# Moving zero products about on TensorE in a fused attention and soft-MoE kernel: three out at the front, ten in at the end

## The chip, the cores and the metric

The kernel runs on one core of a Trainium2 chip. That core has a matrix engine (TensorE, in the profile PE, with its weight loads as PEld), a vector engine (VectorE, DVE), a scalar engine (ScalarE, ACT), a general engine (GpSimd, POOL), a queue for DMAs (SyncE, SP) and 16 DMA engines that all queues share. The metric is the device time of one execution in microseconds; less is better. Each engine works through its own list of instructions in order and waits on semaphores that the others raise.

## The reference

Four sequences of 768 positions go through an attention of 8 heads of 64 columns. Some heads attend to all earlier keys, the others only to 4 "sink" keys and a window of 64. The result, 3072 rows of 512 columns, goes through a soft mixture of experts: each of 32 slots is a softmax-weighted mean over all rows, eight experts of two layers work on four slots each, and each row is a softmax-weighted sum of the slots' results. The core of it:

```python
scores = np.where(mask, q @ k.T / 8, -1e9)           # per head; mask: causal, or sink + window
a = exp(scores - max); a = a / a.sum(-1)             # softmax over the keys
x = (a @ v), heads side by side                      # 3072 x 512
logits = x @ phi                                     # 3072 x 32
slot_input = softmax(logits, over rows).T @ x        # 32 x 512
h = relu(slot_input[e] @ w1[e]); slot_out[e] = h @ w2[e]   # 8 experts, 4 slots each
return softmax(logits, over slots) @ slot_out        # 3072 x 512, float32
```

Inputs and output are float32; the DMAs that POOL issues turn the loads into bf16 on the way, and PE multiplies bf16. The two layers' weights are 32 MB of float32, q, k and v 19 MB, the output 6 MB.

## The kernel before

The attention is cut into 16 "pairs" p = 4b + n of a sequence b and two heads, n and n + 4. For each pair PE makes score blocks (QK), ACT takes their exponentials (EX) into a buffer `pt`, DVE multiplies the blocks that need it by a mask (MK), and PE multiplies by the values (PV.p.i for the six query blocks i = 0 to 5). DVE normalises the result (NM: a reciprocal at L831, then a product at L833), PE transposes it (XT, L845) and DVE or ACT copies the transposes to SBUF (XE). The last pair is cut in halves: PV.15.0 to PV.15.2 go to the first of the two PSUM banks of `pvb`, PV.15.3 to PV.15.5 to the second, and NM.15.0, XT.15.0, XE.15.0 work on the first half, NM.15.3, XT.15.3, XE.15.3 on the second. XT.15.0 and XT.15.3 share one PSUM buffer.

Behind that come the logits of the last sequence (LG), the slots' sums (DS, SA, SI), the first layer (H, L1017), its transposes, and the second layer (W2.e for expert e, L1055). The second layer's last two experts are cut into column halves: W2.6.0 and W2.7.0 make the left 256 columns, W2.6.1 and W2.7.1 the right ones. Each half is scaled into SBUF (SO.0, SO.1; L1113), multiplied with the mixing weights on PE (OM, L1130), scaled by ACT or DVE (OE, L1138 and L1140), and stored (ST, L1149). Twelve of the 24 row tiles go out in left and right halves, the other twelve whole, after the right half is there.

The loads are one queue. POOL issues them in a written order, with waits for the buffers they go to; the last four are the weight halves w14.0, w15.0, w14.1 and w15.1 (L347), for W2.6.0, W2.7.0, W2.6.1 and W2.7.1. SP issues nearly all stores.

The order of everything is made once, when the program is built: a planner (`Plan.run`) places the operations with given costs, start keys and hand-tuned shifts, and the engines' lists follow its order. What an operation emits is not seen by the planner, only its given cost and its number of products.

Some operations emit products with a tile of zeros, `zt`, whose results nobody reads. `fill(n)` (L427) emits n products of 256 columns; TD (the products that make key positions, L432 and L433) begins with fifteen of them and ends with ten, and PE starts with these. ZG are five lone zeros in the first pairs (L511), Z five between the last steps of the slots (L1004). ZT0 and ZT1 (`wait_zeros`, L1073) emit three and two of 448 columns, ZT0 between W2.6.0 and W2.7.0, ZT1 between W2.6.1 and W2.7.1:

```python
def wait_zeros(name, n, key, dep, first=False):
    def emit_z(o):
        for _ in range(n):
            nc.tensor.matmul(banks[zw.slot][:, 0:448], ident, zt, start=True, stop=True)
```

Waits are put in by the framework, by buffers that an instruction writes and reads. For PSUM they can be coarser than the columns touched.

Of the kernel before, what the change touches and what calls it, by code (L numbers as in the profile page):

```python
# [151 lines left out]
def pe(ns, n=1):  # L152
    occ = ns * n / 1000.0
    return {"PE": (occ, occ + 0.27)}
# [72 lines left out]
def kernel(  # L227
# [13 lines left out]
    nc = tc.nc  # L241
# [30 lines left out]
    ident = sb.tile([P, P], BF16, name="ident")  # L272
# [8 lines left out]
    zt = sb.tile([P, 448], BF16, name="zt")  # L281
# [24 lines left out]
    trb = [ps.tile([P, 512], F32, name=f"tr{i}") for i in range(2)]  # L306
    pvb = ps.tile([P, 2, 512], F32, name="pv")

    def tr_bf(s, n):
        return trb[s].bitcast(BF16)[:, 0:n]  # L310
# [14 lines left out]
    def copy_engs(cols, rate=1.75):  # L325
        return {"DVE": (0.035 + cols / rate / 1000.0, 0.2 + cols / rate / 1000.0),
                "ACT": (0.07 + cols / 1200.0, 0.27 + cols / 1200.0)}

    def on(eng, occ, late=0.18):
        return {eng: (occ, occ + late)}  # L330

    def copy(o, dst, src):
        if o.eng == "ACT":
            nc.scalar.copy(dst, src)  # L334
        else:
            nc.vector.tensor_copy(dst, src)  # L336
# [88 lines left out]
    def fill(n):  # L425
        for _ in range(n):
            nc.tensor.matmul(pvb[:, 1, 0:256], zt[:, 0:128], zt[:, 0:256], start=True, stop=True)  # L427

    def emit_td(o):
        fill(15)  # L430
        t = trb[tdb.slot][:, 0:256]
        nc.tensor.matmul(t, unit[:, 0:128], tq, start=True, stop=False)  # L432
        nc.tensor.matmul(t, krow, unit, start=False, stop=True)  # L433
        fill(10)
# [70 lines left out]
    o_zt = pl.op("zt", on("DVE", 0.2), -100, lead=0.7, emit=lambda o: nc.vector.memset(zt, 0.0))  # L505
    tdb = Buf("TR")
    o_td = pl.op("TD", on("PE", 0.6, 0.3), -80, deps=[o_tab], acq=[tdb], emit=emit_td, mode="r32", mm=2)
    o_z = o_zt

# [179 lines left out]
    for b in range(B):  # L689
        for n in range(4):  # L690
            p = 4 * b + n
            k0 = T * p

            tr = Buf("TR")
# [83 lines left out]
    for b in range(B):  # L778
        for n in range(4):
            p = 4 * b + n  # L780
            k0 = T * p
            PVb[p] = Buf("PV")
            last = None
            iorder = [0, 1, 2, 3, 4, 5]

            def pv_at(h, i, p=p):
                return (h, 65 * i) if p < 15 else (i // 3, 195 * h + 65 * (i % 3))

            for i in iorder:
                deps, need = [v2e[p], vfo[p]] + [o_z][p:], set()  # L790
                for j in range(i + 1):
                    if (j, i) == (5, 5):
                        deps.append(exto[p])
                    else:
                        g = PGRP[(j, i)]
                        deps.append(masko[p, g] if i - j <= 1 else expo[p, g])

                def emit_pv(o, b=b, n=n, p=p, i=i, pv_at=pv_at):
                    pT = pTs[PTb[b, n].slot]
                    vb = vbs[VBb[b].slot]  # L800
                    for h in range(2):
                        bk, c = pv_at(h, i)
                        for j in range(i + 1):
                            rhs = vb[:, n, j, h, 0:65] if i - j <= 1 else vfs[VFb[p].slot][:, h, j, 0:65]
                            if (j, i) == (5, 5):
                                lt = ptx[PTXb[b].slot][:, h, n, :]
                            else:
                                lt = pT[:, h, PCOL[(j, i)]:PCOL[(j, i)] + 128]
                            nc.tensor.matmul(pvb[:, bk, c:c + 65], lt, rhs,  # L809
                                             start=(j == 0), stop=(j == i))  # L810

                last = pl.op(f"PV.{p}.{i}", pe(31.5, 2 * (i + 1)), k0 + T - 2.5 + 0.5 * i,
                             deps=list(dict.fromkeys(deps)) + ([last] if last else []),
                             acq=[PVb[p]] if i == 0 else [],
                             rel=[PTb[b, n]] + ([VFb[p]] if i == 5 else []) +
                                 ([PTXb[b], VBb[b]] if i == 5 else []), emit=emit_pv, mode="full", mm=2 * (i + 1))

            pvo = {i: pl.ops[i - 6] for i in range(6)}
            halves = [(0, 6)] if p < 15 else [(0, 3), (3, 6)]
            tr = Buf("TR")  # L820
            xhalf = {}
            for i0, i1 in halves:
                part = f"{p}" if i1 - i0 == 6 else f"{p}.{i0}"

                def emit_nm(o, i0=i0, i1=i1, b=b, n=n, p=p):
                    r = rs[p % 2][:, :, i0:i1]
                    if p < 15:
                        pvw = pvb[:, :, 65 * i0:65 * i1].rearrange("p i (j c) -> p i j c", c=65)
                    else:
                        pvw = pvb[:, i0 // 3, 0:390].rearrange("p (i j c) -> p i j c", i=2, c=65)  # L830
                    nc.vector.reciprocal(r, pvw[:, :, :, 64])  # L831
                    xo = xbs[XBb[b].slot][:, i0:i1, 128 * n:128 * (n + 1)].rearrange("p j (i d) -> p i j d", i=2)
                    nc.vector.tensor_tensor(xo, pvw[:, :, :, 0:64],  # L833
                                            r.rearrange("p i (j o) -> p i j o", o=1).to_broadcast([P, 2, i1 - i0, 64]),
                                            op=ALU.mult)

                normo[p] = pl.op(f"NM.{part}", on("DVE", 0.335 + 0.1333 * (i1 - i0)), k0 + T + 1.0,
                                 deps=[pvo[i1 - 1], XBb[b].op], acq=[XBb[b]] if n == 0 else [], rel=[PVb[p]],
                                 emit=emit_nm)

                def emit_xt(o, i0=i0, i1=i1, b=b, n=n, tr=tr):
                    t = tr_bf(tr.slot, 768)
                    xv = xbs[XBb[b].slot]
                    for i in range(i0, i1):
                        nc.tensor.transpose(t[:, 128 * i:128 * (i + 1)], xv[:, i, 128 * n:128 * (n + 1)], ident)  # L845

                a = pl.op(f"XT.{part}", pe(56, i1 - i0), k0 + T + 2.5, deps=[normo[p]],
                          acq=[tr] if i0 == 0 else [], rel=[XBb[b]], emit=emit_xt, mode="full", mm=i1 - i0)

                def emit_xe(o, i0=i0, i1=i1, n=n, tr=tr):  # L850
                    cs = slice(128 * i0, 128 * i1)
                    copy(o, xT[:, n, cs], tr_bf(tr.slot, 768)[:, cs])

                xhalf[i0] = xto[p] = pl.op(f"XE.{part}", copy_engs(128 * (i1 - i0)), k0 + T + 3.0, deps=[a, o_st, XTb[b].op],
                               acq=[XTb[b]] if n == 0 else [], rel=[tr], emit=emit_xe)
# [213 lines left out]

    def wait_zeros(name, n, key, dep, first=False):  # L1070
        def emit_z(o):
            for _ in range(n):
                nc.tensor.matmul(banks[zw.slot][:, 0:448], ident, zt, start=True, stop=True)  # L1073

        pl.op(name, pe(190, n), key, deps=[dep], acq=[zw] if first else [], rel=[zw], emit=emit_z, mode="full", mm=n)
# [89 lines left out]
    for gi in range(6):  # L1165
        n = dict(halved).get(gi, 0)
# [55 lines left out]
```

## Time and profile before

| | |
|---|---|
| median of 3 runs | 147.77 us (147.71 to 148.36) |
| profiled execution | 147.56 us |
| its span, first to last instruction | 145.8 us |
| PE busy | 124.6 us, 85% of the span |
| DVE, ACT, POOL busy | 110.8, 107.9, 40.5 us |
| moved by DMA | 33.40 MB, HBM read 52.49 MB, written 6.29 MB |
| mean granted TensorE clock | 0.944 |

A row of a timeline has the start in us from the span's first instruction, the duration, the engine, the line of the kernel, the operation, what it writes and reads, the shapes, and how many instructions are merged into the row; in brackets stands how long the engine was idle before it and what ended that. A row of a table of stretches has the stretch, its length, the busy time and number of instructions of PE, PEld, DVE, ACT and POOL, the granted TensorE clock (1.00 is full, 0.50 half), the mean busy share of the DMA engines and the GB/s moved. A row of the chain that ended last has start, duration, and the work; at each step it goes back to what released the next one. "DMA to landing" has the time from a DMA's issue until its data have landed: least, median, most of the DMAs in the stretch. In that view a line's row has durations in ns (least, median, most), and its first and last start.

### The profile page before, as it was taken

What the parts mean: (1) busy time and instruction counts of PE and PEld (TensorE: products, weight loads), DVE (VectorE), ACT (ScalarE), POOL (GpSimd) and SP (SyncE); (2) the same over time, 40 slices, a digit from 0 to 9 for tenths busy, and PEclk for the clock granted to TensorE, in tenths of its full rate; (3) what the DMA queues carried; (4) which work ended last, traced back from release to release, by engine and by line L of the source; (5) the groups of instructions that cost most, each with busy time, mean ns of one, the idle gap of its engine ahead of it and who ended that gap; (6) DMA issues with size and microseconds to landing.
All of it is one profiled execution on the core that took longest, in us unless ns stands there. A gap on an engine that the chain in (4) does not pass through costs nothing.

```text
span 145.8 us, 4941 instructions
## 1 busy us (share of the span) xinstructions
PE 124.6 (85%) x2134; PEld 82.3 (56%) x2134; DVE 110.8 (76%) x254; ACT 107.9 (74%) x147; POOL 40.5 (28%) x73
## 2 busy tenths in 40 slices
PE   6959989999999999999989999999959899869100
PEld 4437566676776758776548766666737355444000
DVE  1796399999999999999799899999983312449700
ACT  3152799999999988999998999999971461549300
POOL 6988631310311470100170011405380000110000
PEclk9985699999999999999999999999995999999965
DMA  5999999999999999999999999999999999999995
GB/s 135 277 208 211 215 215 214 212 216 214 215 214 214 216 215 214 216 214 211 215 214 215 214 216 219 212 217 215 217 210 215 211 194 197 185 321 362 407 420 247
DMA packets 14648, 33.40 MB, mean 229 GB/s; under 512 B 867, under 2 KB 7651, under 8 KB 14115
## 3 DMA queue, kind: packets, MB, share of 16 engines
q0 software_dynamic: 11184, 26.22, 92.9%
q1 hardware_dynamic: 3442, 6.88, 12.7%
q8 instruction: 16, 0.26, 0.6%
q14 instruction: 6, 0.04, 0.1%
HBM read 52.49 MB, written 6.29 MB: 403 GB/s over the span
## 4 chain that ended last, share of the span: by engine, by line
PE 28%; DVE 25%; DMA 18%; ACT 15%; issue 6%; POOL 1%; SPq 0%; DVEq 0%; ACTq 0%; POOLq 0%
DMA qk<-in_moe_w_dram 15%; ACT pt L735 11%; PE sc L665 6%; DVE pt L681 5%; PE pv L809 5%; DVE xv L833 5%; DMA phf<-in_moe_phi_dram 4%; DVE qk L336 3%; PE tr L613 3%; PE tr L639 3%; PE bk L1130 3%; PE tr L872 2%; DVE slot L1140 2%; DVE vf L714 2%; PE tr L845 2%
## 5 line engine op out<-in xcount | busy, mean ns | idle before, releaser
L735 ACT ACTIVATE pt<-sc 128x1024 bf16<-128x1024 f32 x80 | 77.0, 1049 | 3.0 <-PE sc L665 2.8
L665 PE MATMUL sc<-qk 64*128 64x512 bf16 (+3 forms) x256 | 31.3, 311 | 1.2 <-ACT pt L735 0.8
L681 DVE TENSOR_TENSOR pt<-pt,msk 128x1024 bf16<-128x1024 bf16 (+1 forms) x48 | 29.0, 609 | 2.0 <-ACT pt L735 1.8
L809 PEld LDWEIGHTS <-pt 128*128 128x128 bf16 x640 | 23.7, 98 | 6.2 <-issue 5.2
L809 PE MATMUL pv<-vx,pt 128*128 128x65 bf16 x320 | 25.9, 194 | 0.3 <-DVE xv L833 0.2
L809 PE MATMUL pv<-vf,pt 128*128 128x65 bf16 x320 | 21.6, 196 | 0.9 <-DVE xv L833 0.9
L347 POOL DMA_DIRECT2D slot<-in_moe_w_dram x11 | 7.8, 705 | 39.3 <-PE tr L639 29.5
L639 PE MATMUL tr<-ident,slot 128*64 128x128 bf16 (+1 forms) x448 | 16.3, 219 | 0.4 <-ACT qk L334 0.3
L336 DVE COPY qk<-tr 128x768 bf16<-128x768 bf16 (+2 forms) x33 | 15.1, 481 | 1.5 <-PE tr L613 1.3
L639 PEld LDWEIGHTS <-slot 128*64 128x64 bf16 (+1 forms) x448 | 13.1, 109 | 5.1 <-issue 4.8
L833 DVE TENSOR_TENSOR xv<-pv,rs 128x768 bf16<-128x768 f32 (+1 forms) x17 | 15.5, 910 | 0.6
L665 PEld LDWEIGHTS <-qk 64*128 64x128 bf16 x256 | 10.4, 94 | 9.6 <-issue 3.3
L1140 DVE TENSOR_SCALAR slot<-bk,rrow 128x256 f32<-128x256 f32 (+1 forms) x19 | 9.2, 561 | 2.2 <-PE bk L1130 2.2
L896 POOL COPY expT<-eT 128x192 bf16<-128x192 bf16 x12 | 7.4, 657 | 12.2 <-ACT eT L879 12.2
L336 DVE COPY xv<-tr 128x512 bf16<-128x512 bf16 (+2 forms) x20 | 7.9, 409 | 2.4 <-PE tr L613 2.2
L845 PE MATMUL tr<-ident,xv 128*128 128x128 bf16 x96 | 8.4, 224 | 1.3 <-DVE xv L833 0.9
L613 PE MATMUL tr<-ident_u,slot 96*64 96x96 bf16 x192 | 7.3, 238 | 1.9 <-DVE phi L553 1.4
L613 PEld LDWEIGHTS <-slot 96*64 96x64 bf16 x192 | 6.3, 133 | 4.5 <-issue 4.1
L336 DVE COPY xT<-tr 128x768 bf16<-128x768 bf16 (+1 forms) x14 | 7.5, 538 | 1.1 <-PE tr L845 1.1
L1138 ACT ACTIVATE slot<-bk,rrow 128x256 f32<-128x256 f32 (+1 forms) x17 | 7.7, 569 | 0.9 <-PE bk L1130 0.9
L699 PE MATMUL tr<-ident,xv 128*128 128x128 bf16 x96 | 8.1, 220 | 0.0
L845 PEld LDWEIGHTS <-xv 128*128 128x128 bf16 x96 | 6.0, 99 | 2.9 <-DVE xv L833 1.7
(123 smaller groups left out, 169.0 us busy)
## 6 DMA issues: line engine op xcount, KB each, us to landing
slot<-in_moe_w_dram POOLq DMA_DIRECT2D x10, 1024.0 KB, 24.5
out_dram<-slot SPq DMA_DIRECT2D x3, 1024.0 KB, 6.2
out_dram<-slot SPq DMA_DIRECT2D x10, 256.0 KB, 3.2
slot<-in_q_dram POOLq DMA_DIRECT2D x2, 768.0 KB, 19.4
slot<-in_k_dram POOLq DMA_DIRECT2D x2, 768.0 KB, 24.1
qk<-in_moe_w_dram SPq DMA_DIRECT2D x1, 1024.0 KB, 6.1
slot<-in_v_dram POOLq DMA_DIRECT2D x2, 512.0 KB, 21.3
qk<-in_moe_w_dram POOLq DMA_DIRECT2D x1, 1024.0 KB, 17.5
```

What stands on the lines that cost most here:

```text
L336: nc.vector.tensor_copy(dst, src)
L347: acq=[buf] if buf else [], lead=1.3, emit=lambda o: nc.gpsimd.dma_start(dst(), src))
L613: nc.tensor.transpose(t[64 * i:64 * (i + 1), :, :, s, :], rv[:, i, 8 * c + s, :], ident_u)
L639: nc.tensor.transpose(t[64 * i:64 * (i + 1), :, s, :], rv[:, i, 8 * c + s, :], ident[0:R, 0:R])
L665: nc.tensor.matmul(scb[sc.slot][:, i, c:c + 128 * nb], kk, qq.rearrange("p b c -> p (b c)"), start=True, stop=True)
L681: nc.vector.tensor_tensor(pT, pT, mh, op=ALU.mult)
L699: nc.tensor.transpose(t[:, 128 * j:128 * (j + 1)], vT[:, 6 * n + j, :], ident)
L735: nc.scalar.activation(pTs[PTb[b, n].slot][:, :, 512 * g:512 * (g + 1)], scb[sc.slot], ACT.Exp, scale=scale)
L809: nc.tensor.matmul(pvb[:, bk, c:c + 65], lt, rhs, start=(j == 0), stop=(j == i))
L833: nc.vector.tensor_tensor(xo, pvw[:, :, :, 0:64], r.rearrange("p i (j o) -> p i j o", o=1).to_broadcast([P, 2, i1 - i0, 64]), op=ALU.mult)
L845: nc.tensor.transpose(t[:, 128 * i:128 * (i + 1)], xv[:, i, 128 * n:128 * (n + 1)], ident)
L1140: nc.vector.tensor_scalar(d, banks[bf.slot][:, 0:w], sc_, None, op0=ALU.mult)
```

## The change

Four edits in what operations emit; the planner's costs, counts and order are as before.

- TD begins with 12 zeros of 256 columns, before with 15.
- PV.15.3 begins with three zeros of 448 columns into the second bank of `pvb`, ahead of its own eight products.
- XT.14, the transposes of pair 14, begins with three zeros of 448 columns into the transposes' own PSUM buffer.
- ZT0 and ZT1 emit two zeros more each: five and four.

```diff
     def emit_td(o):
-        fill(15)
+        fill(12)
...
                 def emit_pv(o, b=b, n=n, p=p, i=i, pv_at=pv_at):
                     pT = pTs[PTb[b, n].slot]
                     vb = vbs[VBb[b].slot]
+                    if (p, i) == (15, 3):
+                        for _ in range(3):
+                            nc.tensor.matmul(pvb[:, 1, 0:448], ident, zt, start=True, stop=True)
...
-                def emit_xt(o, i0=i0, i1=i1, b=b, n=n, tr=tr):
+                def emit_xt(o, i0=i0, i1=i1, b=b, n=n, p=p, tr=tr):
                     t = tr_bf(tr.slot, 768)
+                    if p == 14:
+                        for _ in range(3):
+                            nc.tensor.matmul(trb[tr.slot][:, 0:448], ident, zt, start=True, stop=True)
...
     def wait_zeros(name, n, key, dep, first=False):
         def emit_z(o):
-            for _ in range(n):
+            for _ in range(n + 2):
                 nc.tensor.matmul(banks[zw.slot][:, 0:448], ident, zt, start=True, stop=True)
```

## The prediction

> **What bounds the kernel now.** I read the page first: its span, the busy times and the DMA row in 40 slices.
>
> ```profile
> span 145.8 us, 4941 instructions
> ...
> PE 124.6 (85%) x2134; PEld 82.3 (56%) x2134; DVE 110.8 (76%) x254; ACT 107.9 (74%) x147; POOL 40.5 (28%) x73
> ...
> DMA  5999999999999999999999999999999999999995
> ```
>
> The profiled execution took 147.56 us, of which 145.8 us are span and 1.76 us lie around it; the median of the runs shown is 147.77 us. The reader should see that the DMA engines are nine tenths busy or more in 38 of 40 slices. No compute engine does that: PE is at 85%, DVE at 76%, ACT at 74% of the span. Next I read the chain that ended last, in order of time.
>
> ```profile
> 108.08 21.34 DMA qk<-in_moe_w_dram
> ...
> 129.46 0.43 PE bk L1055 x8
> ```
>
> The last weight half is asked for at 108.08 and lands 21.34 us later, at 129.42. The last second-layer product (W2.7.1) starts at 129.46, 0.04 us behind it. So is this a long transfer or a long queue? The issues tell:
>
> ```profile
> L347 POOL DMA_DIRECT2D qk<-in_moe_w_dram x2: 873/874/876, 106.3 to 108.1; - x2
> ...
> L347 POOL DMA_DIRECT2D pt<-in_moe_w_dram x1: 873/873/873, 107.2 to 107.2; - x1
> ...
> DMA to landing us min/median/max: 17.8/19.6/21.3
> ...
> L1149 SPq DMA_DIRECT2D out_dram<-slot x1: 372/372/372, 131.4 to 131.4; - x1
> ...
> DMA to landing us min/median/max: 2.7/2.7/2.7
> ...
> L1149 SPq DMA_DIRECT2D out_dram<-slot x3: 344/361/567, 135.1 to 137.6; - x3
> ...
> DMA to landing us min/median/max: 4.9/6.2/7.3
> ```
>
> The last three weight halves are issued at 106.35, 107.21 and 108.08 and land at 124.1 (106.3 + 17.8), 126.8 (107.2 + 19.6) and 129.4: 2.65 us apart, though issued 0.87 us apart. It is a queue. The stores look the same: the first store of right halves needs 2.7 us from issue to landing, the last three, of 1 MB each, 4.9, 6.2 and 7.3 us; they land at 140.0 (135.1 + 4.9) and 144.9 (137.6 + 7.3), 2.45 us apart each. The last store is issued at 137.6, 7.3 us before it lands. Transfers set the end; a compute engine matters only where it lets the transfers run dry. Two places could: PE late for W2.7.1, and the stores of left halves late while the last load is alone in the queue.
>
> **Front, three zeros fewer.** PE runs 15 zeros from the start, then the position products (TD).
>
> ```profile
> 1.15 3.38 PE L427 MATMUL pv<-zt 128*128 128x256 bf16 x15 [1.15 <-DVE zt L505]
> ...
> 4.46 0.10 PEld L432 LDWEIGHTS <-xT 1*128 1x128 bf16 x1 [0.41 <-POOL pc_i L420]
> ...
> 3.28:6.69 3.41, 3.41 (x17) 1.90 (x16) 2.56 (x14) 0.59 (x2) 3.41 (x10) 1.00 0.97 297
> ```
>
> Fifteen in 3.38 us is 0.22 us each, so three fewer end 0.66 us earlier, at about 3.87. TD then starts no sooner: its weight load is released at 4.46 by POOL's last table. Cost 0, gain 0; the work that hides it is POOL's. What goes is 0.6 us of PE activity before 4.46, in a stretch that had 3.41 of 3.41 us busy; 2.8 are left. I take 0, since 2.41 us suffice elsewhere (below). If the full clock were lost for the next stretch, the most that I can read for such a loss is what one costs at 109, 0.8 us (below); PE has 0.43 us to spare at the end, so some 0.4 us would come through. That is the upper end; a lower one under 0 has no row, as TD is held by POOL.
>
> **First pause: three zeros ahead of the transposes of pair 14 (XT.14).**
>
> ```profile
> 104.18 0.55 DVE L336 COPY xT<-tr 128x768 bf16<-128x768 bf16 x1
> ...
> 105.84 0.96 DVE L833 TENSOR_TENSOR xv<-pv,rs 128x768 bf16<-128x768 f32 x1
> ...
> 106.86 0.51 PE L845 MATMUL tr<-ident,xv 128*128 128x128 bf16 x6 [0.92 <-DVE xv L833]
> ...
> 107.80 0.42 DVE L681 TENSOR_TENSOR pt<-pt,msk 128x512 bf16<-128x512 bf16 x1 [0.23 <-ACT pt L735]
> ...
> 107.94 0.22 PE L809 MATMUL pv<-vx,pt 128*128 128x65 bf16 x2
> ...
> 108.20 0.20 DVE L831 RECIPROCAL rs<-pv 128x6 f32<-128x6 f32 x1
> 108.43 0.56 DVE L833 TENSOR_TENSOR xv<-pv,rs 128x384 bf16<-128x384 f32 x1
> 109.05 0.32 PE L809 MATMUL pv<-vf,pt 128*128 128x65 bf16 x3 [0.88 <-DVE xv L833]
> ...
> 127.97 0.55 PE L1073 MATMUL bk<-zt,ident 128*128 128x448 bf16 x2
> ...
> 129.46 0.40 PE L1055 MATMUL bk<-qk,xT 128*32 128x256 bf16 x8 [0.95 <-DMA qk<-in_moe_w_dram]
> ...
> 124.04 0.74 PE L1073 MATMUL bk<-zt,ident 128*128 128x448 bf16 x3
> 124.71 0.40 PE L1055 MATMUL bk<-qk,xT 128*32 128x256 bf16 x8
> ```
>
> Two zeros of 448 columns take 0.55 us and three 0.74 us, so one more costs 0.19 us at the full clock. XT.14 waits 0.92 us on PE for the normalisation that runs 105.84 to 106.80. The zeros need only a PSUM buffer whose readers are done with the copy at 104.18 (until 104.73), so three of them (0.74 us, until about 106.65) lie wholly in the wait. Cost 0; the cover is that normalisation, and without it they would cost 0.57.
>
> **Second pause: three zeros ahead of PV.15.3.** Here the wait does not stand where the zeros stand. The twenty products of PV.15.0 to PV.15.3 run through until 108.16; the 0.88 us wait is in front of the next ones, PV.15.4, at 109.05. It ends with the normalisation NM.15.0 (reciprocal at 108.20, product 108.43 to 108.99). In the program as built NM.15.0 waits for the count that the last product of PV.15.3 raises, not PV.15.2, although it reads the other bank. So zeros ahead of PV.15.3 push PV.15.3, and NM.15.0 behind it, and PV.15.4 behind that: 3 x 0.19 = 0.57 us on the chain, not hidden. NM.15.0 also waits for the mask that ends at 108.22, 0.06 us after PV.15.3, so about 0.5 could be the least; at half clock it is more. I take 0.57.
>
> **What the pauses may give back.** After them PE runs at half clock for one stretch:
>
> ```profile
> 105.68:109.09 3.41, 1.59 (x34) 1.12 (x29) 2.94 (x6) 2.63 (x3) 3.27 (x4) 1.00 1.05 210
> 109.09:112.50 3.41, 3.22 (x50) 2.56 (x50) 0.90 (x3) 0.48 (x1) 0.00 (x0) 0.50 1.05 213
> ...
> 126.17:129.58 3.41, 2.41 (x25) 1.07 (x25) 2.27 (x6) 2.23 (x6) 1.33 (x2) 1.00 1.10 231
> 129.58:132.99 3.41, 3.19 (x36) 1.94 (x30) 2.48 (x7) 2.61 (x7) 0.00 (x0) 1.00 1.04 369
> ...
> 104.55 0.26 PE L809 MATMUL pv<-vf,pt 128*128 128x65 bf16 x3
> ...
> 105.20 0.19 PE L809 MATMUL pv<-vx 128*128 128x65 bf16 x1
> ...
> 110.16 0.24 PE L809 MATMUL pv<-vx 128*128 128x65 bf16 x1
> ...
> 111.00 0.58 PE L1004 MATMUL sc<-zt,ident 128*128 128x448 bf16 x1
> 111.77 0.48 PE L845 MATMUL tr<-ident,xv 128*128 128x128 bf16 x3 [0.19 <-ACT xT L334]
> ```
>
> The stretch with 1.59 us busy was followed by a granted clock of 0.50 (109.09 to 112.50); the one with 2.41 us (126.17 to 129.58) by 1.00. With the zeros the first has about 1.59 + 0.65 + 0.57 = 2.8, so I expect the full clock to stay. Then the 22 products of PV.15.4 and PV.15.5 take the 0.84 us of pair 14 (104.55 to 105.39) in place of 1.35 us (109.05 to 110.40): 0.51 less. Six transposes take 0.51 us at the full clock, three take 0.48 at the half, so two groups of three (XT.15.0, XT.15.3) save some 0.15 each, an estimate from these two rows. Sum on the chain: +0.57 - 0.51 - 0.30 = -0.24 us. The logits, slots and first layer behind it move 0.24 us forward: none waits for a load there.
>
> The Trainium skill, TensorE: Matmul & The Clock Gate, section "What's actually happening", has the clock fall back after at least one idle window of about 3.4 us, and calls the window free-running. The trace agrees with the length (109.09 to 112.50) but not with the idleness: the stretch before the drop had 1.59 us of work in it. By that rule 0.9 us pauses are harmless and filling them gives nothing: the sum would be +0.57 in place of -0.24, the first rival below.
>
> **Two more zeros in each late wait.** ZT0 (three zeros at 124.04) stands ahead of W2.7.0, whose weights have landed at 124.1. W2.7.0 starts at 124.71 only because of the zeros: five of them make it 2 x 0.19 = 0.38 later, on the chain to the left halves. With -0.24 that is +0.14 us: W2.7.0 at 124.85. ZT1 (two zeros at 127.97) stands ahead of the 0.95 us wait for the last load: PE was done at 128.51. It is now done at 128.51 + 0.14 + 0.38 = 129.03, still 0.43 us before 129.46. Cost 0; the cover is the load, and if PE comes later than 129.46, each further 1 us of delay is 1 us on the right stores.
>
> What do left stores 0.14 us later cost?
>
> ```profile
> 125.50:126.00 0.50, 0.31 (x3) 0.28 (x3) 0.00 (x0) 0.14 (x1) 0.00 (x0) 1.00 1.50 195
> ...
> 127.00:127.50 0.50, 0.49 (x4) 0.22 (x3) 0.50 (x2) 0.50 (x2) 0.40 (x2) 1.00 1.00 135
> 127.50:128.00 0.50, 0.50 (x11) 0.16 (x10) 0.50 (x3) 0.50 (x3) 0.50 (x1) 1.00 0.93 159
> ```
>
> With two loads in the queue 195 GB/s move, with the last alone 135 and 159: of 1.0 us, (60 + 36) / 2 / 195 = 25% is lost. So 0.14 us more of that is 0.04 us. The bounds are 0 (the last load lands sooner when nothing competes) and 0.14. I take 0.04.
>
> **Sum.** 0 + 0 + 0.04 + 0 = +0.04 us: 147.60 against the profiled 147.56, and 147.8 against the median of 147.77. The planner's order and every load's issue stay as they are. No instruction is moved past a queue; PE alone has 14 more instructions (7 products and their weight loads).
>
> **Rivals.**
> First, the clock is not kept: the half clock follows whatever PE does in the pauses, or the stretches lie elsewhere against the work in other executions. Then the chain is 0.57 us later, W2.7.0 at 125.66, and PE reaches W2.7.1 at 128.51 + 0.57 + 0.76 = 129.84: 0.38 us late, one for one on the right stores. Time 147.77 + 0.38 = 148.15. For it: one drop in one execution is little to read a bound from; against: 2.41 us sufficed later. The Trainium skill's page above would have this case by both of its statements.
> Second, slower: the added zeros themselves run at half clock. The zero at 111.00 took 0.58 us where one at the full clock takes about 0.36 (0.74 - 2 x 0.19), so each added one would cost about twice 0.19, 0.38 us. Three on the chain and four in the waits are 7 x 0.38 = 2.66 us of delay; the wait of 0.95 us covers the first part, and 1.7 us remain: 149.5. It decides from 0.95 us of total delay; over 0.5% (0.74 us, about what a measurement here can tell from no change) needs 1.69 us. For it: the half clock begins right at 109.09, some 0.3 us behind PV.15.3. Against: at 124 to 129 the granted clock was 1.00.
> Third, faster: the chain gains more than 0.38 us, left stores start earlier and fill the 25% hole. At most the 0.25 us lost between 127 and 128 comes back: 147.5, within 0.5%. For more, the load queue itself would have to run faster, and no edit touches it.
>
> **How the numbers follow.** Forecast, no change, 147.4 to 148.0 by itself: 0.55. Clock not kept, 148.0 to 148.4: 0.17. Zeros at half clock, or another delay that brings PE more than 1.69 us late, over 148.5: 0.20. Faster: 0.08, of which by its price 0.03 lie within 0.5% and 0.05 I leave for a load queue that runs quicker for a reason I do not see. So faster by over 0.5%: 0.05; within: 0.55 + 0.17 + 0.03 = 0.75; slower: 0.20. The range 147.2 to 148.7 takes in the first two cases, the bounds of the front (+0.4) and of the hole (-0.25), and the near edge of the slow case.
>
> **What would show it.** Right: TD still at about 4.46; the zeros done before XT.14; NM.15.0's reciprocal near 108.77 and PV.15.4 near 109.6; granted clock 1.00 from 109 to 112.5; W2.7.0 near 124.85; W2.7.1 still released by the load, after a wait of about 0.4 us; stores landing back to back. Wrong: W2.7.1 not released by a DMA, or the last load landing at another time than 129.4, or a stretch of half clock at another place; a shift of all compute before 105 would point to the front.

## The result, and the profile after

The changed kernel takes 149.2 us (median of 6 runs, 148.94 to 149.89) against 147.76 us before (median of 6, 147.59 to 148.36). The ratio is 1.0098, with a 95% interval of 1.0073 to 1.0123: slower by 1.4 us. The forecast was no change, 147.8 us in a range from 147.2 to 148.7. The profiled execution of the changed kernel took 149.89 us, the longest of its six, of which 148.1 us are span and 1.79 us lie around it.

The code has moved by some lines: zeros of ZT0 and ZT1 are at L1079 (before L1073), W2 at L1061 (L1055), XT at L851 (L845) with its zeros at L848, PV at L812 (L809) with its zeros at L803, NM's product at L836 (L833), the stores at L1155 (L1149).

First the page. Of the kernel before, two rows that the prediction did not show, the GB/s in 40 slices and the queue of instructions:

```profile
GB/s 135 277 208 211 215 215 214 212 216 214 215 214 214 216 215 214 216 214 211 215 214 215 214 216 219 212 217 215 217 210 215 211 194 197 185 321 362 407 420 247
...
q8 instruction: 16, 0.26, 0.6%
```

The same page of the changed kernel, with the span and the busy times:

```profile
span 148.1 us, 4955 instructions
...
PE 126.7 (86%) x2141; PEld 82.9 (56%) x2141; DVE 110.3 (74%) x254; ACT 107.9 (73%) x147; POOL 40.4 (27%) x73
...
GB/s 142 274 207 210 217 212 217 210 217 211 214 215 215 216 214 215 215 214 214 214 215 215 218 212 216 215 213 212 217 212 216 201 197 199 173 349 354 376 427 131
...
q8 instruction: 17, 0.28, 0.7%
```

The span is 2.3 us longer. PE is busy 2.1 us longer and has seven more products. The row of the GB/s shows where the time lies: the last slices. And one row has changed that the prediction never looked at: the queue of instructions, q8, has 17 packets where it had 16. These packets are the program itself, fetched for an engine; they travel over the same DMA engines as loads and stores.

Next the places that the prediction named, on PE and DVE in the timeline of the changed kernel:

```profile
4.45 0.39 PE L432 MATMUL tr<-xT 1*128 1x256 bf16 x1 [0.56 <-POOL xT L419]
...
106.64 0.74 PE L848 MATMUL tr<-zt,ident 128*128 128x448 bf16 x3
107.63 0.51 PE L851 MATMUL tr<-ident,xv 128*128 128x128 bf16 x6 [0.24 <-DVE xv L836]
...
108.53 0.73 PE L803 MATMUL pv<-zt,ident 128*128 128x448 bf16 x3
...
110.39 0.25 PE L812 MATMUL pv<-vf,pt 128*128 128x65 bf16 x3 [0.88 <-DVE xv L836]
...
109.54 0.20 DVE L834 RECIPROCAL rs<-pv 128x6 f32<-128x6 f32 x1 [0.55 <-PE pv L812]
...
124.54 1.12 PE L1079 MATMUL bk<-zt,ident 128*128 128x448 bf16 x5
125.59 0.40 PE L1061 MATMUL bk<-qk,xT 128*32 128x256 bf16 x8
...
128.84 0.93 PE L1079 MATMUL bk<-zt,ident 128*128 128x448 bf16 x4
130.09 0.40 PE L1061 MATMUL bk<-qk,xT 128*32 128x256 bf16 x8 [0.32 <-DMA qk<-in_moe_w_dram]
```

TD is released by POOL as before. XT.14's zeros fill the pause and leave 0.24 us of it. DVE's reciprocal of NM.15.0 now waits 0.55 us for PE, where PV.15.3 stands behind its zeros. ZT0 and ZT1 have five and four products, and W2.7.1 still waits for the last load, for 0.32 us. So up to 130.09 this is the forecast, shifted. Then the last load, in the chain that ended last:

```profile
108.84 21.21 DMA qk<-in_moe_w_dram
```

And the last three stores, by their line (durations in ns, first and last start, and the time from issue to landing):

```profile
L1155 SPq DMA_DIRECT2D out_dram<-slot x3: 344/345/964, 137.0 to 138.2; - x3
...
DMA to landing us min/median/max: 5.3/7.1/9.0
```

The last load lands at 108.84 + 21.21 = 130.05; before it was 129.42. That is 0.63 us later. The last of the three last stores lands at 138.2 + 9.0 = 147.2; before, 144.87. That is 2.33 us later. So 1.70 us appear behind the last load, while nothing but stores moves. The table of stretches shows how they appear (its last two columns are the DMA engines' share and the GB/s). The kernel before:

```profile
144.00:144.50 0.50, 0.00 (x0) 0.00 (x0) 0.00 (x0) 0.00 (x0) 0.00 (x0) 0.50 0.40 164
144.50:145.00 0.50, 0.00 (x0) 0.00 (x0) 0.00 (x0) 0.00 (x0) 0.00 (x0) 0.50 0.00 0
```

The same table of the changed kernel:

```profile
137.00:137.50 0.50, 0.00 (x0) 0.00 (x0) 0.50 (x2) 0.00 (x0) 0.00 (x0) 1.00 0.31 105
145.00:145.50 0.50, 0.00 (x0) 0.00 (x0) 0.00 (x0) 0.00 (x0) 0.00 (x0) 0.50 0.93 393
145.50:146.00 0.50, 0.00 (x0) 0.00 (x0) 0.00 (x0) 0.00 (x0) 0.00 (x0) 0.50 0.09 33
146.00:146.50 0.50, 0.00 (x0) 0.00 (x0) 0.00 (x0) 0.00 (x0) 0.00 (x0) 0.50 0.04 16
146.50:147.00 0.50, 0.00 (x0) 0.00 (x0) 0.00 (x0) 0.00 (x0) 0.00 (x0) 0.50 0.04 16
```

Before, the DMA engines go from a share of 0.40 to nothing. After, they are at 0.93 until 145.5 and then at 0.09, 0.04 and 0.04, with the last packet ending at 146.87. One engine of 16 is a share of 0.0625, so this is the picture of one engine that still has work when the others are done.

The trace has a second record of this: sixteen landings for every store, as many as there are DMA engines. Of the last store of the kernel before, all sixteen came between 144.55 and 144.87. Of the last store of the changed kernel, fifteen came between 145.89 and 146.09 and the sixteenth at 147.20, 1.11 us behind the fifteenth. So most of the 1.70 us is one part in sixteen that is late. The other 0.6 us is common to all: the fifteenth comes 16.04 us behind the last load, before 15.43.

That common part goes with a gap at 137.0 to 137.5, where the share is 0.31. The stores that SP issues tell more (durations of an issue in ns, least, median, most); the kernel before:

```profile
L1149 SPq DMA_DIRECT2D out_dram<-slot x13: 344/447/662, 127.3 to 137.6; - x13
```

The changed kernel:

```profile
L1155 SPq DMA_DIRECT2D out_dram<-slot x13: 344/446/1382, 128.2 to 138.2; - x13
```

One issue took 1.38 us, where before none took more than 0.66. It is the one that starts at 135.48; the three stores behind it are issued from 137.04 on, and by then the DMA engines have run dry.

### The profile page after: what moved, and what is told of

It is laid out like the page before. It is cut to its first block, busy times and chain, and to the rows that moved or that the text cites. A ratio compares the mean times of both kernels' runs of the same rounds, so it can differ in the third digit from the quotient of the medians.

```text
span 148.1 us, 4955 instructions
## 1 busy us (share of the span) xinstructions
PE 126.7 (86%) x2141; PEld 82.9 (56%) x2141; DVE 110.3 (74%) x254; ACT 107.9 (73%) x147; POOL 40.4 (27%) x73
## 4 chain that ended last, share of the span: by engine, by line
PE 28%; DVE 25%; DMA 18%; ACT 14%; issue 5%; POOL 1%; SPq 0%; DVEq 0%; ACTq 0%; POOLq 0%
DMA qk<-in_moe_w_dram 14%; ACT pt L735 10%; PE sc L665 6%; DVE pt L681 5%; PE pv L812 5%; DVE xv L836 5%; DMA phf<-in_moe_phi_dram 4%; DVE qk L336 3%; PE tr L613 3%; PE tr L639 3%; PE bk L1136 2%; PE tr L878 2%; DVE slot L1146 2%; DVE vf L714 2%; PE tr L851 2%
## 5 line engine op out<-in xcount | busy, mean ns | idle before, releaser
L812 PEld LDWEIGHTS <-pt 128*128 128x128 bf16 x640 | 23.4, 97 | 6.4 <-issue 5.2
L812 PE MATMUL pv<-vx,pt 128*128 128x65 bf16 x320 | 25.6, 193 | 0.3 <-DVE xv L836 0.2
L812 PE MATMUL pv<-vf,pt 128*128 128x65 bf16 x320 | 21.2, 194 | 0.9 <-DVE xv L836 0.9
L836 DVE TENSOR_TENSOR xv<-pv,rs 128x768 bf16<-128x768 f32 (+1 forms) x17 | 15.5, 910 | 0.6
L613 PEld LDWEIGHTS <-slot 96*64 96x64 bf16 x192 | 6.9, 142 | 3.7 <-issue 3.3
L851 PE MATMUL tr<-ident,xv 128*128 128x128 bf16 x96 | 8.1, 219 | 0.8 <-ACT xT L334 0.4
L613 PE MATMUL tr<-ident_u,slot 96*64 96x96 bf16 x192 | 8.0, 251 | 0.9 <-DVE phi L553 0.4
L714 DVE TENSOR_TENSOR vf<-vx,fmx 128x528 bf16<-128x528 bf16 x16 | 7.1, 442 | 0.6 <-ACT vx L334 0.5
```

The source lines that it names most:

```text
L613: nc.tensor.transpose(t[64 * i:64 * (i + 1), :, :, s, :], rv[:, i, 8 * c + s, :], ident_u)
L714: nc.vector.tensor_tensor(vfs[VFb[p].slot], vv, fmx[:, n], op=ALU.mult)
L812: nc.tensor.matmul(pvb[:, bk, c:c + 65], lt, rhs, start=(j == 0), stop=(j == i))
L836: nc.vector.tensor_tensor(xo, pvw[:, :, :, 0:64], r.rearrange("p i (j o) -> p i j o", o=1).to_broadcast([P, 2, i1 - i0, 64]), op=ALU.mult)
```

## The experiments

The suspicion from the page: the program of PE is longer by 14 instructions (4297 in PE's list as built, 4283 before), the seventeenth piece of it is therefore fetched inside the run, at 135.49 in this trace, and that fetch, 16 KB in 0.93 us, takes a DMA engine from the stores of the end. (The page counts 4268 and 4282 products and weight loads; 15 more instructions of the list are not counted as busy.) The rivals are those of the prediction: the later compute, the clock, the zeros in the waits. The table collects all runs; the text behind it takes them one by one. "Load to store" is the time from the landing of the last load to the landing of the last store, in the profiled execution, as worked out above for the two kernels; the fetches are the packets of q8 within the span, with the start and duration of the last. Medians and ratios are those of the comparison of each kernel with the one before on the same chip, where the median before was 147.56 to 147.89 us; the ratio is the one on record with its interval, not the quotient of two medians.

| kernel | PE instr. | fetches, last at (took) | load to store, us | median, us | ratio to before (95%) |
|---|---|---|---|---|---|
| e3: front 12 | 4277 | 16, 122.06 (0.94) | 15.63 | 147.64 | 1.0006 (0.9981 to 1.0030) |
| e8: no ZT0 | 4277 | 16, 121.52 (0.94) | 15.58 | 147.98 | 1.0000 (0.9976 to 1.0023) |
| before | 4283 | 16, 124.53 (0.96) | 15.45 | 147.76 | |
| e2: change, front 5 | 4283 | 16, 124.42 (0.95) | 15.46 | 147.94 | 1.0021 (0.9994 to 1.0047) |
| e10: 3 zeros at the end | 4289 | 16, 124.24 (0.95) | 15.47 | 147.72 | 1.0010 (0.9982 to 1.0039) |
| e4: waits alone | 4291 | 16, 122.97 (0.89); another behind the span | 15.49 | 148.23 | 1.0039 (1.0008 to 1.0069) |
| e6: pauses alone | 4295 | 17, 139.77 (0.96) | 17.04 | 148.15 | 1.0006 (0.9978 to 1.0034) |
| after | 4297 | 17, 135.49 (0.93) | 17.15 | 149.2 | 1.0098 (1.0073 to 1.0123) |
| e1: 7 zeros at the end | 4297 | 17, 136.89 (0.88) | 17.13 | 149.37 | 1.0108 (1.0058 to 1.0158) |
| e5: pauses and waits | 4303 | 17, 133.87 (0.88) | 16.43 | 149.13 | 1.0086 (1.0052 to 1.0120) |
| e7: split front zeros | 4333 | 17, 133.40 (0.93) | 16.31 | 148.99 | 1.0077 (1.0052 to 1.0102) |
| e9: 137 small at the end | 4557 | 17, 136.21 (0.96) | 16.81 | 148.64 | 1.0070 (1.0043 to 1.0097) |
| e11: 180 small at the end | 4643 | 18, 136.94 (0.96) and 143.93 (0.95) | 17.18 | 149.74 | 1.0119 (1.0084 to 1.0154) |

The kernels without a fetch under the last stores need 15.45 to 15.63 us from load to store, those with one 16.31 to 17.18. Nothing lies between.

**The program's length alone (e1).** The kernel before, with seven zeros behind the last output product on PE, where nothing waits for them:

```diff
+    oms = [o for o in order if o.name.startswith("OM.")]
+    for _ in range(7):
+        nc.tensor.matmul(banks[oms[-8].acq[0].slot][:, 0:448], ident, zt, start=True, stop=True)
```

> The kernel before with seven zero products of 448 columns behind the last output product on TensorE, where nothing waits for it: the same number of TensorE instructions as in the changed kernel, none of its edits. Theory A (the added instructions lengthen TensorE's program over a boundary, and one more fetch of 16 KB of instructions holds up a DMA engine under the last stores): about 149.0 us, a fetch of 16 KB on queue 8 near 135 to 137 us, 17 fetches in place of 16, the last stores some 1.2 to 1.7 us late. Theory B (compute comes later, by the zeros and the lost clock at the front, and the left stores with it): 147.8 us as before, since no compute is touched.

Measured: 149.37 against 147.69 us, ratio 1.0108 (1.0058 to 1.0158). PE's list ahead of the end is that of the kernel before, and the whole loss is there. One row of its page:

```profile
q8 instruction: 17, 0.28, 0.7%
```

And its table of stretches at the end:

```profile
144.00:144.50 0.50, 0.00 (x0) 0.00 (x0) 0.00 (x0) 0.00 (x0) 0.00 (x0) 0.50 0.40 164
144.50:145.00 0.50, 0.00 (x0) 0.00 (x0) 0.00 (x0) 0.00 (x0) 0.00 (x0) 0.50 0.08 33
145.00:145.50 0.50, 0.00 (x0) 0.00 (x0) 0.00 (x0) 0.00 (x0) 0.00 (x0) 0.50 0.04 16
145.50:146.00 0.50, 0.00 (x0) 0.00 (x0) 0.00 (x0) 0.00 (x0) 0.00 (x0) 0.50 0.04 16
```

Up to 144.5 the share is that of before, 0.40, and where before has 0.00 there follow 0.08, 0.04 and 0.04. Most of the engines end when those of the kernel before end; a share of about one engine carries on. Of the last store, fifteen landings came between 144.53 and 144.78, the sixteenth at 146.31.

**The whole change at the old length (e2).** The changed kernel, with seven zeros fewer in front of TD:

```diff
-        fill(12)
+        fill(5)
```

> The changed kernel with the front's zeros cut from 12 to 5, so that TensorE's program is as long as before; the six zeros in the pauses and the four in the waits stay. Theory A: 16 fetches, no late last stores, 147.6 to 148.4 us. Theory B: 149.2 us or more, since the front is no warmer and the zeros of the pauses and waits are all there.

Measured: 147.94 against 147.69 us, ratio 1.0021 (0.9994 to 1.0047). Pauses, waits and all are there, and most of the loss is gone, perhaps all: by the interval at most 0.5% of the time remains, where the whole change cost 1.0%. (One of its ten runs took 149.2 us with a span of 147.4; of that run there is no trace.) One row of its page:

```profile
q8 instruction: 16, 0.26, 0.7%
```

And its table of stretches at the end:

```profile
144.50:145.00 0.50, 0.00 (x0) 0.00 (x0) 0.00 (x0) 0.00 (x0) 0.00 (x0) 0.50 0.17 66
145.00:145.50 0.50, 0.00 (x0) 0.00 (x0) 0.00 (x0) 0.00 (x0) 0.00 (x0) 0.50 0.00 0
```

Sixteen fetches, and no thin tail: 0.17 and then nothing; all sixteen landings of the last store came between 144.97 and 145.44. e1 and e2 together decide it: the length without the change costs 1.1%, the change without the length nothing that is clear of zero.

**The front alone (e3).**

```diff
-        fill(15)
+        fill(12)
```

> The kernel before with 12 zeros at the front in place of 15, nothing else. Theory A: no 17th fetch, 147.8 us. Theory B: the clock reaches full speed one stretch later, compute is some 0.8 us late at 105 us, left stores late: 148.4 to 149.0 us.

Measured: 147.64 us, ratio 1.0006 (0.9981 to 1.0030). In the profiled execution compute ran 2 us ahead of the kernel before: XT.14 behind its 0.92 us wait started here at 104.82, before at 106.86. Its timeline of PE, with W2.7.1 at the end:

```profile
104.82 0.51 PE L845 MATMUL tr<-ident,xv 128*128 128x128 bf16 x6 [0.92 <-DVE xv L833]
...
129.18 0.40 PE L1055 MATMUL bk<-qk,xT 128*32 128x256 bf16 x8 [0.43 <-DMA qk<-in_moe_w_dram]
```

The last load landed at 129.13 all the same, and the time did not move. Two microseconds of compute won are worth nothing here, as the prediction said. That 0.77 us lost, by which the changed kernel was late at the same place, cost nothing does not follow from that. Other executions tell: e1 and e5 have the loss with XT.14 at 105.63 and 106.68, no later than before; e10 has no loss with XT.14 at 107.28, 0.42 us later than before.

**The waits alone (e4).**

```diff
-            for _ in range(n):
+            for _ in range(n + 2):
```

> The kernel before with two more zeros in each of the two late waits, nothing else (8 more TensorE instructions). Theory A: 147.8 us if 8 instructions stay below the boundary, 149.0 if they cross it; the number of fetches tells. Theory B: W2.7.0 0.38 us later, left stores 0.38 us later, 147.9 to 148.2 us.

Measured: 148.23 us, ratio 1.0039 (1.0008 to 1.0069). The two waits are not what costs: W2.7.0 and W2.7.1 both waited for their loads, 1.03 and 1.09 us, and load to store was 15.49 us. The profiled execution took 149.44 us with a span of 146.3, so 3.1 us lie around the span instead of 1.8; the seventeenth packet of q8 came at 148.51, behind the last store. In other runs of this kernel 1.8 to 2.8 us lie around it. With 4291 instructions the fetch falls at the very end of the program, and the long time around the span goes with it; that it is the fetch that is timed there is read from this one trace.

**Pauses and waits, front as before (e5).** The changed kernel with the front put back:

```diff
-        fill(12)
+        fill(15)
```

> The changed kernel with 15 zeros at the front again: pauses and waits alone, 20 TensorE instructions more than before. Theory A (a 17th fetch of instructions holds up a DMA engine under the last stores): 149.2 us, 17 fetches, the last one three output products earlier than in the changed kernel, near 134.5 to 135.5. Theory B (late compute): about 148.2 us, as the front is as before.

Measured: 149.13 against 147.89 us, ratio 1.0086 (1.0052 to 1.0120). With six instructions more than the change the fetch comes at 133.87, and the loss is there.

**The pauses alone (e6).** The kernel before with the three zeros of PV.15.3 and the three of XT.14, as in the change's diff.

> The kernel before with the three zeros in each of the two pauses alone, 12 TensorE instructions more. Theory A: 148.8 to 149.4 us, 17 fetches, the last just as TensorE ends its products; 148.2 if it falls behind the span as with 8 instructions more. Theory B: the zeros ahead of PV.15.3 cost 0.57 us on compute that waits for loads later: 147.8 us.

Measured: 148.15 us, ratio 1.0006 (0.9978 to 1.0034), with runs from 147.27 to 149.1. The profiled execution is the 149.1: it has the seventeenth fetch at 139.77 and 17.04 us from load to store. The fastest runs are as fast as before. The spans on record say more. Nine of the ten runs have 145.5 to 146.7 us, as the kernel before has in its runs beside them (145.5 to 146.9); only the profiled one has 147.3. Three of the nine have 2.1 to 3.4 us around the span, as e4 has. That suggests that at 4295 instructions the fetch falls under the stores in some executions and behind them in others; only the one trace shows it.

**The fetch without any zero moved (e7).** The kernel before, with the front's 15 and 10 zeros of 256 columns made 30 and 20 of 128, so that the work in the front is about the same and the list is 50 instructions longer:

```diff
+    def fill2(n):
+        for _ in range(n):
+            nc.tensor.matmul(pvb[:, 1, 0:128], zt[:, 0:128], zt[:, 0:128], start=True, stop=True)
...
-        fill(15)
+        fill2(30)
...
-        fill(10)
+        fill2(20)
```

> The kernel before with the 15 and 10 front zeros of 256 columns replaced by 30 and 20 of 128 columns: 50 TensorE instructions more in the same time, so the 17th fetch falls some 18 output products earlier than in the changed kernel, near 131 us, when left stores fill the queue. Theory A: 148.6 to 149.4 us, with the stores behind the fetch late by some 1.7 us; if the moment matters, less, 147.8 to 148.4. Theory B: 147.8 us.

Measured: 148.99 us, ratio 1.0077 (1.0052 to 1.0102). Compute was 2.4 us earlier than before at XT.14 (104.50), no pause is filled and no wait is lengthened, and load to store took 16.31 us. The extra instructions stand in the first 7 us and the cost is paid in the last 15: what counts is the length of the list, not where it grows. Against the kernels without such a fetch, the one at 133.40 costs 0.7 to 0.9 us, e5's at 133.87 0.8 to 1.0, and those at 135.5 and later 1.2 to 1.7.

**ZT0 away (e8).** The kernel before without ZT0's three zeros (the planner's count is kept):

```diff
-            for _ in range(n):
+            for _ in range(n if n > 1 else 0):
...
-                wait_zeros(f"ZT{c}", 2 if c else 3, kt + (29.5 + e if c else 22.5), w2o[c], c == 0)
+                wait_zeros(f"ZT{c}", 2 if c else 1, kt + (29.5 + e if c else 22.5), w2o[c], c == 0)
```

> The kernel before without ZT0, the three zeros ahead of W2.7.0: left halves and their stores some 0.57 us earlier, 16 fetches. If the stretch with one load alone in the queue loses a quarter of the transfer, as the prediction had it: 147.5 to 147.6 us. If the transfers lose nothing there: 147.7 us.

Measured: 147.98 us, ratio 1.0000 (0.9976 to 1.0023). The left stores began at 126.26 where they began at 126.78 before, and the time did not move. By the term that the prediction gave to the hole (0.25 us of lost time per 1.0 us) this would be 0.13 us, and the interval is 0.35 us to either side: the term is neither shown nor refuted. The kernels also differ in more than the hole: in this execution the granted clock was 0.50 from 125.97 to 136.21, under the output products, and load to store was 15.58 us all the same. So a half clock there is not what costs either (e10 had it from 130.94 to 134.36, with 15.47 us).

**How much of the list is under the stores (e9, e10, e11).** The kernel before with three zeros of 448 columns (e10, as e1), or 137 (e9) or 180 (e11) of 32 columns, at the end of PE's list; for 137:

```diff
+    oms = [o for o in order if o.name.startswith("OM.")]
+    for _ in range(137):
+        nc.tensor.matmul(banks[oms[-8].acq[0].slot][0:32, 0:32], zt[:, 0:32], zt[:, 0:32], start=True, stop=True)
```

> The kernel before with three zero products behind the last output product: 6 TensorE instructions more, two fewer than in the run with the late waits alone, whose 17th fetch came behind the span. Theory A: 16 fetches and 147.8 us if the boundary lies above, some 148.2 us with a wide spread if it lies at the end of the program as there. Theory B: 147.8 us.

> The kernel before with 137 tiny zero products (32 columns) behind the last output product: 274 TensorE instructions more, so an 18th fetch of instructions, about 256 instructions behind the 17th. Theory A1 (each fetch holds one DMA engine, and the next fetch goes to another; the end waits for the engine that is furthest behind): no worse than with the 17th alone, 149.0 to 149.4 us. Theory A2 (fetches hold up all transfers, or the same engine each time): twice the loss, about 150.4 us. Theory B (no fetch matters): 147.8 us.

> The kernel before with 180 tiny zero products behind the last output product, 360 TensorE instructions more, so that an 18th fetch comes some 256 instructions behind the 17th, near 139 us, still under the last stores; with 137 the 18th had not come. Theory A1 (each fetch holds one DMA engine, the next one another, and the end waits for the engine that is furthest behind): about 148.7 us, as with the 17th alone. Theory A2 (the same engine, or all transfers, each time): about 149.8 us. Theory B (no fetch matters): 147.6 us.

Measured: three zeros, 4289 instructions, ratio 1.0010 (0.9982 to 1.0039), no seventeenth fetch in the span; 137, 4557 instructions, ratio 1.0070 (1.0043 to 1.0097), one fetch under the stores, and the eighteenth that was expected did not come; 180, 4643 instructions, ratio 1.0119 (1.0084 to 1.0154), an eighteenth at 143.93. Three added zeros cost nothing measurable, seven cost 1.1%, and with 137 it is no more than with seven. So it is not the work of the products or their number that costs, but a boundary in the list. The next one lies between 4557 and 4643 instructions, that is 260 (4557 less 4297) to 354 (4643 less 4289) behind the first. The list's length decides, and in all thirteen profiled executions a fetch under the stores, the thin tail and the long time from load to store come together.

That the fetch holds up one DMA engine is shown by the landings of the last store. In the six executions without such a fetch its sixteen landings lie within 0.19 to 0.55 us. In the six with one, fifteen lie within 0.20 to 0.60 us and the sixteenth comes 0.86 (e7) to 1.59 us (e6) behind them. In e11, with two fetches, two are late: fourteen come between 144.15 and 145.00, the others at 146.05 and 146.35. The packet records agree: in e6 about sixteen packets of data are under way at any time in the microsecond before the fetch, fifteen while it runs, and sixteen again behind it.

A fetch also goes with a late issue where SP is issuing stores. SP's longest issue of a store took 0.87 to 1.38 us in the six executions whose fetch came before SP was through, and at most 0.68 us in the others, e6 among them, whose fetch came after the last issue.

What a second fetch adds to the time is not settled. Of the two theories put down for e11, the two late landings show two engines held up, as A1 has it, but the median of 149.74 us is near the 149.8 of A2, not the 148.7 of A1. Every run of e11 (148.92 to 150.44 us) is longer than every run of e9 (148.51 to 148.89), which was run on another chip, yet e11's interval overlaps with those of e9 and e1.

No kernel here is faster than the one before; e2, e3, e6, e8 and e10 equal it within their intervals.

## Why the prediction was wrong, point by point

**The step that failed** is in the sum: "No instruction is moved past a queue; PE alone has 14 more instructions (7 products and their weight loads)". They were counted, and costed at nothing. They carry the list over a boundary between 4289 and 4297 instructions, a seventeenth fetch runs under the last stores and holds up one DMA engine, and load to store takes 17.15 us instead of 15.45: +1.70 in the profiled executions; e1, which has this term alone, measures +1.7 in the medians (0.9 to 2.3 by its interval), and the whole change +1.4. The row that could have raised the question stood on the page: 16 packets of instructions, on the engines that set the end. How near the list was to a boundary is in no row of the trace of before. An estimate from the 256 instructions of a block in the Trainium skill, Runtime: NRT & Kernel Launch, section "Instruction fetch mechanics", is 14 / 256, a chance of one in 18 of crossing one, if nothing is known of the place; even that was not in the forecast. The third rival said of the load queue that "no edit touches it"; the longer list puts one more transfer on the DMA engines that loads and stores use.

**Front.** TD starts at 4.45, released by POOL, as forecast. The clock came later. The group of PE's products of L613 between 6.8 and 10.1 us (count, then busy time and mean ns), before:

```profile
L613 PE MATMUL tr<-ident_u,slot 96*64 96x96 bf16 x16 | 0.5, 209 | 0.0
```

After:

```profile
L613 PE MATMUL tr<-ident_u,slot 96*64 96x96 bf16 x16 | 0.8, 281 | 0.0
```

They took 281 ns in place of 209. (The granted clock reads 1.00 there in the changed kernel too, but in that trace the record of it starts only at 19.07; the durations tell.) Compute was 0.77 us late at XT.14 (107.63 against 106.86). The prediction had bounded that at some 0.4 us coming through at the end. Whether three zeros fewer make it late is not shown: e3 has the same twelve zeros and XT.14 at 104.82, e2 has five and 106.98, and the nine executions with the front of before have 104.72 to 107.28. W2.7.1 waited for its load all the same.

**First pause.** Right: the zeros ran 106.64 to 107.38 within the wait, and XT.14 waits for DVE as before.

**Second pause.** Right, in place and size: PV.15.4 comes 1.34 us later (109.05 to 110.39), of which 0.77 were there at XT.14; 0.57 remain, as forecast.

**Clock kept.** Right in this execution. Its row of stretches:

```profile
109.09:112.50 3.41, 2.15 (x55) 1.83 (x54) 1.51 (x4) 0.61 (x2) 0.63 (x1) 1.00 1.07 216
```

The granted clock is 1.00, where it was 0.50 before. The last slots' product came 0.49 us later than before (113.57 to 114.06); less 0.77 that is -0.28 from the pauses, where -0.24 was forecast. But that the zeros kept the clock is not shown. In the four executions with zeros in the pauses it did not fall between 105 and 113 us; without them it fell there in three (the kernel before, e3 and e9) and not in the six others. The one drop that the forecast was read from was the rarer case, so that it came out right may be luck. The stretches of 3.41 us lie elsewhere in each execution (the record of the full clock starts at 6.69 us before, at 19.07 in the changed kernel and at 8.54 in e3), so the same zeros need not gain this each time; and e3 and e8, with XT.14 two microseconds earlier and no gain, show that time won on this chain does not reach the end.

**Waits.** W2.7.0 starts 0.88 us later (124.71 to 125.59): 0.77 - 0.28 + 0.39; the forecast +0.38 for ZT0 is right. W2.7.1 is released by the DMA with 0.32 us to spare, where 0.4 was forecast. ZT1 is hidden. The hole's +0.04 is far below what these runs can tell (e8).

**The last load** landed at 130.05 instead of 129.42. The prediction named this as a sign of error. In all profiled executions it lands between 129.13 and 130.19. The four kernels with longer waits (the changed one, e2, e4, e5) have 129.83 to 130.05, the others 129.13 to 129.48 and once 130.19 (e7). That may be the waits or the execution: the spans of the kernel before, in its 25 runs beside e1, also range from 145.5 to 146.5 us. By its interval e2, which has all four edits at the old length, is at most 0.5% slower; whether the longer waits cost some tenths of a microsecond stays open. The 0.63 us is about the 0.7 us by which the profiled run lies above its median.

**The rivals.** Of the two slower ones, neither occurred: the clock was kept, and the zeros ran at full clock (0.73 and 0.74 us for three). The slower end came by a way that was not among them. So the chance of 0.20 for slower stood for the wrong mechanism.

## What to carry to other kernels

Count the instructions of each engine's list, not only their time. Where the end of a kernel is bound by DMA, a list that grows past a fetch boundary puts one more transfer under it, whatever the added instructions do; look at the packets of the instruction queue and at the time of the last one before adding anything, and test a change of emitted instructions at equal length (as in e2), or with the length alone (as in e1). A kernel whose runs spread between two times (e6) may stand on the boundary.

## What the runs showed of the hardware that was not expected

- A fetch of instructions is a packet of 16 KB on the DMA engines, 0.88 to 0.97 us long for the last ones within the spans; the last two lie 7 to 17 us apart there. Under the last stores one of them costs 0.7 to 1.7 us of the end, which can be more than its own length. In all seven profiled executions with such a fetch the stores end with two or more half-microseconds at a DMA share of 0.04 to 0.13; in the six others there is at most one such. One of the sixteen landings of the last store is then late by 0.86 to 1.59 us, two with two fetches. Which engine makes a fetch is not in the trace, and why a later one costs more than an earlier one, and more than its own length, stays open; in e6 the first packet of a store that begins as the fetch ends took 0.67 us, where its neighbours took 0.31. The Trainium skill, Runtime: NRT & Kernel Launch, section "Instruction fetch mechanics", says that a sequencer refills its store of instructions in blocks of 16 KiB, 256 instructions, over a DMA queue of its own while it executes, and that crossing a block's boundary is "mostly hidden". The traces agree with the size. For the distance, the runs give 260 to 354 of the counted instructions, just above the page's 256. To the stores at the end it is not hidden, with +1.0% in the changed kernel and +1.1% in e1.
- A fetch at the very end of the program seems to lengthen what is timed without being in the span: 3.1 us around the span instead of 1.8 in e4, with the packet at 148.51 and the last store landed at 145.35.
- The stretches of the clock begin elsewhere in each execution, and a stretch with 2.39 us of work of 3.42 (6.69 to 10.11, kernel before) was followed by half clock where 2.41 of 3.41 (126.17 to 129.58) was not. The table of stretches of the kernel before:

```profile
6.69:10.11 3.42, 2.39 (x32) 1.38 (x31) 2.83 (x9) 1.89 (x4) 3.42 (x7) 1.00 1.12 208
10.11:13.50 3.39, 2.40 (x38) 1.55 (x39) 2.98 (x9) 0.91 (x2) 2.50 (x6) 0.50 1.12 208
```

The bound that the prediction read from the second alone does not hold. That agrees with what the Trainium skill, TensorE: Matmul & The Clock Gate, section "What's actually happening", says of a free-running window, and not with its idle window as the condition for the fall.
